# Attention's first batch: three head pairs in two halves of blocks, the first halves of all of them first

## The chip, the core and the metric

The kernel runs on one core of a Trainium2 chip. The time is device microseconds of one execution; a lower number is better.

## What is computed

The reference is a windowed attention followed by two gated layers. The weights come as 64-bit floats, q, k and v as 32-bit floats.

```
q, k, v: (4 batches, 8 heads, 576 tokens, 64)
scores = q @ k^T / 8, ALiBi slope per head, only 0 <= query - key < 128
x  = softmax(scores) @ v                  # to (2304 tokens, 512)
x  = (silu(x @ w_gate) * (x @ w_val)) @ w_out      # 512 -> 1536 -> 512
g  = x @ w_in;  out = (g * cos(g)) @ w_out2        # 512 -> 2048 -> 512
```

## The kernel before, in words

**Attention.** Two heads make a pair `u`; there are 16 pairs, four in each batch, and pairs 0 to 3 are the first batch. A pair's 576 tokens are four blocks of 128 (`NB = 4`) and a tail of 64. An item `(u, h, i)` is one block `i` of head `h`; the tails of both heads are one more item, `i = NB`. So a pair has nine items, and there are 144. A program loop, `for n in range(...)`, goes over them, and in round `n` it writes instructions for items at different stages: scores on TensorE (`do_s`, tiles `s`, L512), bias and row maximum on VectorE (`do_bias`, L520), exponential on ScalarE two items later (`do_exp`, L529), sum, reciprocal and scaling (L535, L541, L554 on GpSimd), transposes on TensorE five items later (`do_t`, L573; L563 in the later batches), a copy to SBUF by ScalarE (`do_hi`, L591), and attention times v eight or nine items later (`do_pv`, tile `pv` at L631, the tail at L605 and L607). ScalarE then writes the result's high part `xh` (L637) and VectorE its rest `xl` (L640). Every engine runs its own instructions in the written order.

**A pair's preparation** stands in the rounds of the pair before it: q is loaded and turned (`prep_t`, L449) and scaled to `qx` (`prep_q`, L455), the tail is turned (L461, L469, L471), k is turned and copied to `kx` (`prep_k`, L458). All loads are issued by SyncE in written order (`load_qk` L391 and L396, six issues; `load_v` L407 and L411, three issues). `nat1` holds two pairs' q and k, `nat2` two pairs' v, and `qk` two pairs' turned q and k.

**Weights.** A generator, `convert` (one step per round), turns the 64-bit weights into pairs of 32-bit parts, nine tiles of 512 KB: gate 0, val 0, gate 1, val 1, gate 2, val 2, out 0, out 1, out 2. Each is loaded by SyncE into one of two buffers `st` (L95, L100) and begins on ScalarE with L130 and L132, goes over VectorE (L133 to L145) and GpSimd (L152, L167) and ends as `wh` and `wl`.

**The filler.** Between attention's instructions TensorE gets work of the next layer: a generator of steps, each of three matmuls (L84, L85, L86). A batch has 72 steps (`STEPS`) in two jobs. The first batch's first job takes tokens 0 to 255: 12 steps of gate (`a_l1`), 12 of val and 12 of out (`a_l2`). Its first eight gate steps go by pairs of heads, and two of them run as soon as `ready` holds that pair, that is, when `xh` and `xl` of its tokens 0 to 255 are written. The second job needs the whole batch (`release`). `run_fill` writes at most what has come due; at most 1.6 steps come due in a round (`RATE`), and while a batch is worked on, `rate` spreads the steps that are left evenly over the rounds until the next batch is released. What remains after attention runs behind it, and then come the remaining layers, which the change does not touch.

**What sets the order in the first batch.** Pairs follow one another, nine items each. Only pair 3 (`u == NP - 1`) multiplies by v in two parts: tokens 0 to 255 when its first four items are through, then the rest. The stage distances are constants (`TRANS`, `HIGH`, `PVS`), one or two less for pair 3.

Of the kernel before, what the change touches and what calls it, by code (L numbers as in the profile page):

```python
# [9 lines left out]
F32 = mybir.dt.float32  # L10
F32R = mybir.dt.float32r
U32 = mybir.dt.uint32
AF = mybir.ActivationFunctionType
# [15 lines left out]
def kernel(  # L29
# [12 lines left out]
    nc = tc.nc  # L42
# [358 lines left out]
    def load_v(u):  # L401
        if u >= U:
            return
        b, p = divmod(u, NP)
        t = nat2.tile([128, NB, 2, D], F32, tag="v", name="v")
        for h in range(2):
            nc.sync.dma_start(  # L407
                out=t[:, :NB, h, :],
                in_=v[b, 2 * p + h, :NB * 128, :].rearrange("(n s) d -> s n d", s=128),
            )  # L410
        nc.sync.dma_start(  # L411
            out=vtail[u % 3][128 - TAIL:], in_=v[b, 2 * p:2 * p + 2, NB * 128:, :].rearrange("h s d -> s h d")
        )
        nat["v", u] = t


    vtail = [const.tile([128, 2, D], F32, name=f"vtail{j}") for j in range(3)]
    for t in vtail:
        nc.vector.memset(t[:128 - TAIL], 0.0)
    load_qk(0)  # L420
# [4 lines left out]
    load_v(0)  # L425
    ident = const.tile([128, 128], F32, name="ident")
    make_identity(nc, ident)
    qtx = [const.tile([128, 128], F32, name=f"qt{j}") for j in range(2)]
# [35 lines left out]
    def prep_tail(u):  # L464
        ps = PQ.pop((u, "t"))
        KT[u] = qk_p.tile([128, S], F32, tag="kx", name="kx")
        for j in range(2):
            r = slice(64 * j, 64 * j + 64)
            nc.scalar.activation(out=qtx[u % 2][r, r], in_=ps[r, 0:64], func=AF.Copy,  # L469
                                 scale=qscale[r, u % NP:u % NP + 1])  # L470
        nc.scalar.copy(out=KT[u][:, NB * 128:S], in_=ps[:, 64:128])  # L471

    items, first, final = [], {}, {}
    for u in range(U):
        for i in range(0, NB, 2):
            for h in range(2):
                items += [(u, h, i), (u, h, i + 1)]
        items.append((u, 0, NB))
        for j in range(0, NI, 2):
            g = list(range(u * NI + j, u * NI + min(j + 2, NI)))  # L480
            first[g[0]] = final[g[-1]] = g
    N = len(items)
    E, ST, PT, SP, TT, FT = {}, {}, {}, {}, {}, {}

# [3 lines left out]
    def do_s(groups):  # L488


        todo = []
        for g in groups:
            ps = ps_s.tile([128, 512], F32, tag="s", name="s")
            st = stats[stat_turn[0] % len(stats)]
            stat_turn[0] += 1
            at, ops = 0, []
            for m, n in enumerate(g):
                u, h, i = items[n]
                w = width(i)
                o = ps[:, at:at + w]  # L500
                at += w
                if i == NB:
                    ops.append((o, qtx[u % 2], KT[u][:, S - w:S]))
# [78 lines left out]
    def do_hi(g):  # L582
        ps = PT.pop(g[0])
        u, h, i = items[g[0]]
        if i == NB:
            nc.scalar.copy(out=ptt, in_=ps)
            return
        if i == 0:
# [9 lines left out]
    def do_pv(n):  # L598
        u, h, i = items[n]
        b_, p = divmod(u, NP)  # L600
        if i == NB:
            vt = nat["v", u]
            ps = (pm.tile([128, 512], F32, tag="pm", name="pm") if u == NP - 1 else
                  ps_q.tile([128, 512], F32, tag="pq", name="pq"))[:, :128]
            nc.tensor.matmul(out=ps, lhsT=vt[:, NB - 1].rearrange("p h d -> p (h d)"),  # L605
                             rhs=ptt[:, 0:128], start=True, stop=False)
            nc.tensor.matmul(out=ps, lhsT=vtail[u % 3].rearrange("p h d -> p (h d)"),  # L607
                             rhs=ptt[:, 128:256], start=False, stop=True)

            def fin():  # L610
# [67 lines left out]
    def last_pair(n):  # L678

        return 0 <= n < N and items[n][0] == NP - 1  # L680

    def staged(n, late, early):

        if last_pair(n - early) and n - early in final:
            return final[n - early]
        return None if last_pair(n - late) else final.get(n - late)
    for n in range(N + PVS + 2):
        pace = rate(n, due) if n < N else 1.5 * RATE
        due += 0.7 * pace
        u, idx = divmod(n, NI)  # L690
        v1 = u + 1 if u + 1 < U else None

        def ended(j):
            return final.get(n - j)

        todo = list(post)
        post.clear()
        if u < U and idx in AHEAD:
            do_s([first[u * NI + j] for j in AHEAD[idx]])
        turned, high = staged(n, TRANS, 4), staged(n, HIGH, 5)  # L700
        if high:
            do_hi(high)
        for m in first.get(n - EXP, ()):
            do_exp(m)
        for m in first.get(n if idx == NI - 1 else n - 1, ()) if idx else ():
            do_bias(m)
        if ended(NORM):
            do_guard(ended(NORM))
        if turned:
            do_t(turned)  # L710
        if v1 is not None:
            if idx == TT0:
                g = turned
                prep_tail_t(v1, TT[g[0]] if g else ps_t.tile([128, 512], F32, tag="t", name="t"))
        if ended(NORM):
            do_recip(ended(NORM))
            for m in ended(NORM):
# [2 lines left out]
            fn()  # L720
        due -= run_fill(int(due))
        due += 0.3 * pace
        for back in (PVS + 1, PVS, PVS - 2):
            for m in (ended(back) or ())[-1:]:
                u_, h_, i_ = items[m]
                if (h_ == 1 and (i_ == NB - 1 or i_ == 1 and last_pair(m)) or i_ == NB) and back == (
                        PVS - 2 if last_pair(m) else PVS if i_ == NB - 1 else PVS + 1):
                    do_pv(m)
        if v1 is not None:
            if idx == Q0 + 1:  # L730
                prep_q(v1)
            if idx == Q0:
                prep_t(v1, "q")
            if idx == K0:
                prep_t(v1, "k")
            if idx == K0 + 1:
                prep_k(v1)
            if idx == TT0 + 1:
                prep_tail(v1)
            if idx == max(TT0, K0) + 1:  # L740
                load_qk(u + 2)
            if idx == 7:
                load_v(u + 1)
        pdue = min(pdue + 1.0, 1.0)
        while pool_bg and pdue > 0:
            cost, fn = pool_bg.popleft()
# [556 lines left out]
```

## Time and profile before

| | |
|---|---|
| median of 3 runs | 984.19 us (983.91 to 987.03) |
| the profiled execution | 987.27 us, its span 985.2 us |
| mean granted TensorE clock in it | 0.990 |
| TensorE busy | 962.3 us, 98% |
| ScalarE, VectorE, GpSimd busy | 594.9, 731.0, 483.5 us |

A busy share is a mean over stages with different limits, and the busy time of matmuls counts their pipeline's length, so a TensorE that is busy to 90% can still be waiting. The granted clock is in shares of 2.4 GHz: 0.50 is the level of 1.2 GHz. Idle time stands with the instruction that ended it.

### The profile page before, as it was taken

Reading aid. Unit: us, or ns where it says so; the run is one execution under the profiler, and the core shown is the slowest. Engines: PE = TensorE matmul, PEld = TensorE weight load, DVE = VectorE, ACT = ScalarE, POOL = GpSimd, SP = SyncE. Lnnn points to the kernel's source line nnn. Section 1 sums busy time; section 2 is a strip of 40 time slices with the busy share of each in tenths; the row PEclk is TensorE's granted clock in tenths of the full one; section 3 lists DMA queues with packets and bytes.
Section 4 is the critical chain, followed back from the end, with each engine's and each line's share of the span. In section 5 each row is a group of like instructions: output and inputs, shape, how many; then the busy total and the mean of one; then the engine's idle time right before and its main releaser. Section 6 shows DMA issues by size and latency. Waiting matters only on the chain.

```text
span 985.2 us, 17051 instructions
## 1 busy us (share of the span) xinstructions
PE 962.3 (98%) x5620; PEld 884.6 (90%) x5620; DVE 731.0 (74%) x1549; ACT 594.9 (60%) x1366; POOL 483.5 (49%) x567
## 2 busy tenths in 40 slices
PE   6889999999999999999999999999999999999998
PEld 4658888889999999999999999888988888888886
DVE  6767777766288988989989755889666796666664
ACT  6876666653254545555545433878677776777663
POOL 5666645652245667769679721544232442323221
PEclk8889999999999999999999999999999999999999
DMA  7531352322383646647557625865767656576552
GB/s 181 157 92 42 95 123 68 85 75 70 110 281 107 204 128 223 205 130 252 172 164 240 193 89 177 296 201 182 245 201 229 201 161 203 181 247 202 164 180 86
DMA packets 145159, 163.65 MB, mean 166 GB/s; under 512 B 64688, under 2 KB 105648, under 8 KB 144816
## 3 DMA queue, kind: packets, MB, share of 16 engines
q1 hardware_dynamic: 143872, 162.27, 52.6%
q8 instruction: 45, 0.74, 0.3%
q10 hardware_dynamic: 1200, 0.30, 0.1%
q14 instruction: 42, 0.34, 0.1%
HBM read 126.88 MB, written 35.65 MB: 165 GB/s over the span
## 4 chain that ended last, share of the span: by engine, by line
PE 91%; DVE 3%; ACT 2%; DMA 2%; issue 1%; SPq 1%; POOL 0%; DVEq 0%; POOLq 0%; ACTq 0%
PE l L86 13%; PE l L85 13%; PE l L84 13%; PE pm L84 8%; PE pm L85 8%; PE pm L86 8%; PE pm L1028 6%; PE pm L1029 6%; PE pm L1027 5%; PE s L512 3%; PE pv L631 3%; PE pq L449 1%; PE t L563 1%; PE t L573 1%; ACT e L529 1%
## 5 line engine op out<-in xcount | busy, mean ns | idle before, releaser
L1152 POOL TENSOR_TENSOR r<-r,c 128x384 f32<-128x384 f32 x96 | 105.1, 1095 | 248.9 <-ACT r L1150 163.3
L84 PE MATMUL pm<-xh,wh 128*128 128x384 f32 (+3 forms) x456 | 153.4, 336 | 1.5 <-ACT fu L263 1.5
L85 PE MATMUL pm<-xl,wh 128*128 128x384 f32 (+3 forms) x456 | 145.9, 320 | 0.0
L86 PE MATMUL pm<-xh,wl 128*128 128x384 f32 (+3 forms) x456 | 145.9, 320 | 0.0
L86 PE MATMUL l<-wo,hl 128*128 128x512 f32 x288 | 114.2, 396 | 0.0
L85 PE MATMUL l<-wo,hh 128*128 128x512 f32 x288 | 113.7, 395 | 0.0
L84 PE MATMUL l<-wo,hh 128*128 128x512 f32 x288 | 112.1, 389 | 1.2 <-DMA wo<-wod 1.2
L843 POOL TENSOR_TENSOR cs<-cs,st 128x512 uint32<-128x512 uint32 x56 | 79.6, 1421 | 56.9 <-DVE cs L841 49.8
L1028 PE MATMUL pm<-xl,ws 128*128 128x384 f32 x318 | 107.4, 338 | 0.0
L1029 PE MATMUL pm<-xh,ws 128*128 128x384 f32 x318 | 106.8, 336 | 0.0
L1027 PE MATMUL pm<-xh,ws 128*128 128x384 f32 x318 | 106.2, 334 | 0.0
L84 PEld LDWEIGHTS pm<-xh,wh 128*128 128x128 f32 x456 | 86.3, 189 | 6.0 <-issue 2.7
L554 POOL TENSOR_SCALAR e<-e,st 128x128 f32<-128x128 f32 (+1 forms) x144 | 61.1, 427 | 62.1 <-DVE st L541 42.1
L85 PEld LDWEIGHTS pm<-xl,wh 128*128 128x128 f32 x456 | 86.4, 190 | 0.0
L86 PEld LDWEIGHTS pm<-xh,wl 128*128 128x128 f32 x456 | 86.2, 189 | 0.0
L1142 ACT ACTIVATE a<-c 128x384 f32<-128x384 f32 x96 | 49.8, 519 | 53.1 <-DVE c L1168 53.1
L529 ACT ACTIVATE e<-e,st 128x256 f32<-128x256 f32 (+1 forms) x144 | 68.1, 475 | 19.0 <-DVE st L520 13.5
L1147 DVE SCALAR_TENSOR_TENSOR r<-a,r 128x384 f32<-128x384 f32 x96 | 76.7, 799 | 3.3
L1149 ACT ACTIVATE r<-r 128x384 f32<-128x384 f32 x96 | 50.5, 526 | 41.3 <-DVE r L1147 41.3
L84 PE MATMUL l<-uh,wh 128*128 128x384 f32 x216 | 72.6, 336 | 0.7 <-DVE acc L968 0.5
L86 PE MATMUL l<-uh,wl 128*128 128x384 f32 x216 | 72.2, 334 | 0.0
L85 PE MATMUL l<-ul,wh 128*128 128x384 f32 x216 | 72.2, 334 | 0.0
(177 smaller groups left out, 2604.9 us busy)
## 6 DMA issues: line engine op xcount, KB each, us to landing
ws<-wid SPq DMA_DIRECT2D x168, 256.0 KB, 2.8
wo<-wod SPq DMA_DIRECT2D x48, 512.0 KB, 5.2
st<-in_moe_w_out_dram SPq DMA_DIRECT2D x28, 512.0 KB, 3.8
st<-in_moe_w_in_dram SPq DMA_DIRECT2D x16, 512.0 KB, 3.7
st<-in_moe_w_gate_dram SPq DMA_DIRECT2D x12, 512.0 KB, 4.2
st<-in_moe_w_val_dram SPq DMA_DIRECT2D x12, 512.0 KB, 3.8
wid<-sh SPq DMA_DIRECT2D x24, 256.0 KB, 4.0
wid<-sl SPq DMA_DIRECT2D x24, 256.0 KB, 3.5
```

Source lines behind the costliest of these rows:

```text
L84: nc.tensor.matmul(out=ps, lhsT=ah, rhs=bh, start=start, stop=False)
L85: nc.tensor.matmul(out=ps, lhsT=ah, rhs=bl, start=False, stop=False)
L86: nc.tensor.matmul(out=ps, lhsT=al, rhs=bh, start=False, stop=stop)
L529: nc.scalar.activation(out=e[:, :w], in_=e[:, :w], func=AF.Exp, bias=st[:, m:m + 1], scale=-1.0, accum_out=st[:, 2 + 2 * m:3 + 2 * m])
L554: nc.gpsimd.tensor_scalar(e[:, :w], e[:, :w], st[:, 8 + m:9 + m], 1.0, ALU.mult, ALU.mult)
L843: nc.gpsimd.tensor_tensor(out=ti, in0=ti, in1=st[:, :, 0], op=ALU.add)
L1027: nc.tensor.matmul(out=o, lhsT=wh, rhs=xh_, start=start and kk == 0, stop=False, skip_group_check=True)
L1028: nc.tensor.matmul(out=o, lhsT=wh, rhs=xl_, start=False, stop=False, skip_group_check=True)
L1029: nc.tensor.matmul(out=o, lhsT=wl, rhs=xh_, start=False, stop=kk == 1, skip_group_check=True)
L1147: nc.vector.scalar_tensor_tensor(out=r, in0=a, scalar=-C2, in1=r, op0=ALU.mult, op1=ALU.add)
L1149: nc.scalar.activation(out=r, in_=r, func=AF.Abs)
L1152: nc.gpsimd.tensor_tensor(out=r, in0=r, in1=h, op=ALU.mult)
```

## The change

The items of pairs 1 to 3 are put in another order: the first halves (blocks 0 and 1 of both heads, four items) of pairs 1, 2 and 3, then their second halves (blocks 2 and 3 and the tail, five items each). Each half is multiplied by v by itself. Pair 0 and the batches behind it keep their order. Preparation and loads of the first pairs stand in tables of rounds now, and more buffers hold what lives longer: v, turned q and k, and tails of four pairs. The number of items, of loads and of filler steps stays.

```diff
-    nat2 = att.enter_context(tc.tile_pool(name="nat2", bufs=2))
-    qk_p = att.enter_context(tc.tile_pool(name="qk", bufs=2))
+    nat2 = att.enter_context(tc.tile_pool(name="nat2", bufs=4))
+    qk_p = att.enter_context(tc.tile_pool(name="qk", bufs=4))
...
-    items, first, final = [], {}, {}
-    for u in range(U):
-        for i in range(0, NB, 2):
+    items, first, final, part, scores = [], {}, {}, {}, {}
+    HB = NB // 2
+    order = [(0, 0, NB + 1)] + [(u, *c) for c in ((0, HB), (HB, NB + 1)) for u in range(1, NP)]
+    for u, b0, b1 in order + [(u, 0, NB + 1) for u in range(NP, U)]:
+        base = len(items)
+        for i in range(b0, min(b1, NB), 2):
             for h in range(2):
                 items += [(u, h, i), (u, h, i + 1)]
...
-        lo, hi = (0, NB * 128) if u != NP - 1 else (0, HA) if i == 1 else (HA, NB * 128)
+        lo, hi = part[n][0] * 128, min(part[n][1], NB) * 128
...
-    AHEAD = {0: (0, 2), 4: (4, 6), 7: (8,)}
-    Q0, K0, TT0 = 2, 5, 4
+    Q0, K0, TT0 = {1: 2, 2: 8, 3: 12, 4: 28}, {1: 5, 2: 11, 3: 15, 4: 31}, {1: 4, 2: 10, 3: 14, 4: 30}
+    LQ, LV = {2: 1, 3: 6, 4: 20, 5: 33}, {1: 7, 2: 10, 3: 14, 4: 34}
+    for u in range(NP + 1, U):
+        Q0[u], TT0[u], K0[u] = ((u - 1) * NI + j for j in (2, 4, 5))
+        LV[u] = (u - 1) * NI + 7
+        if u + 1 < U:
+            LQ[u + 1] = (u - 1) * NI + 6
...
+    def lag(n):
+
+        u, _, i = items[n]
+        if u in (0, *range(NP, U)):
+            return TRANS, HIGH, PVS + (i == NB)
+        if u == NP - 1 or part[n][0] == 0:
+            return TRANS - 1, HIGH - 1, PVS - 2
+        return TRANS, HIGH, PVS - 1 + (u == 1 and i == NB)
...
-            ps = (pm.tile([128, 512], F32, tag="pm", name="pm") if u == NP - 1 else
+            ps = (pm.tile([128, 512], F32, tag="pm", name="pm") if NP - 2 <= u < NP else
```

What the tables hold: `Q0`, `K0` and `TT0` are the rounds in which a pair's q, k and tail are turned, `LQ` and `LV` those in which its loads are issued. Before, q and k of pairs 2 and 3 were loaded in rounds 6 and 15 and turned from rounds 11 and 20 on.

**SyncE's queue.** Its issues at the start, from pair 0's tail of v to the weight tile val 1. Before:

```order
L411 DMA vtail_128<-in_v_dram 64x2x64
L95 DMA st<-in_moe_w_gate_dram 128x4x256
L391 DMA q<-in_q_dram 128x4x64 x2
L391 DMA k<-in_k_dram 128x4x64 x2
L396 DMA qkt<-in_q_dram 64x2x64
L396 DMA qkt<-in_k_dram 64x2x64
L407 DMA v<-in_v_dram 128x4x64 x2
L411 DMA vtail_129<-in_v_dram 64x2x64
L95 DMA st<-in_moe_w_val_dram 128x4x256
```

The same place in the change, from behind pair 0's tail of v:

```order
L391 DMA q<-in_q_dram 128x4x64 x2
L391 DMA k<-in_k_dram 128x4x64 x2
L396 DMA qkt<-in_q_dram 64x2x64
L396 DMA qkt<-in_k_dram 64x2x64
L95 DMA st<-in_moe_w_gate_dram 128x4x256
L391 DMA q<-in_q_dram 128x4x64 x2
L391 DMA k<-in_k_dram 128x4x64 x2
L396 DMA qkt<-in_q_dram 64x2x64
L396 DMA qkt<-in_k_dram 64x2x64
L407 DMA v<-in_v_dram 128x4x64 x2
L411 DMA vtail_129<-in_v_dram 64x2x64
L95 DMA st<-in_moe_w_val_dram 128x4x256
```

Pair 2's six issues moved ahead of the tile gate 1, and pair 3's six stand between gate 1 and val 1.

**TensorE in rounds 29 and 30.** The names are tiles (`pm` and `xh`, `wh` the filler's, `t` transposed exponentials, `s` scores). Before, the block of filler steps that is shown stands in round 39, between the turning of pair 5's q (round 38) and the scores of round 40:

```order
L449 MATMUL pq<-ident,q 128x128 x4
L573 MATMUL t<-ident,e 128x128 x2
L84 MATMUL pm<-xh,wh 128x256
L85 MATMUL pm<-xl,wh 128x256
L86 MATMUL pm<-xh,wl 128x256
L84 MATMUL pm<-xh,wh 128x256
L85 MATMUL pm<-xl,wh 128x256
L86 MATMUL pm<-xh,wl 128x256
L84 MATMUL pm<-xh,wh 128x256
L85 MATMUL pm<-xl,wh 128x256
L86 MATMUL pm<-xh,wl 128x256
L512 MATMUL s<-kx,qx 128x256 x4
```

In the change it stands in round 29, behind the scores of pair 2's tail:

```order
L520 MATMUL s<-kx,qt_169 128x192
L581 MATMUL t<-ident,e 128x128 x4
L84 MATMUL pm<-xh,wh 128x256
L85 MATMUL pm<-xl,wh 128x256
L86 MATMUL pm<-xh,wl 128x256
L84 MATMUL pm<-xh,wh 128x256
L85 MATMUL pm<-xl,wh 128x256
L86 MATMUL pm<-xh,wl 128x256
L84 MATMUL pm<-xh,wh 128x256
L85 MATMUL pm<-xl,wh 128x256
L86 MATMUL pm<-xh,wl 128x256
L581 MATMUL t<-ident,e 128x128 x2
```

The block of three steps with which the filler gets going (its seventh to ninth step) moved from round 39 to round 29.

**TensorE around the end of the first batch.** In the change, from pair 3's second product with v (round 41) to the filler's 25th step (round 43); its 24th stands in round 39:

```order
L639 MATMUL pv<-pth_974,v 64x128
L639 MATMUL pv<-pth_1021,v 64x128
L639 MATMUL pv<-pth_974,v 64x256
L639 MATMUL pv<-pth_1021,v 64x256
L639 MATMUL pv<-pth_974,v 64x128
L639 MATMUL pv<-pth_1021,v 64x128
L613 MATMUL pm<-ptt,v 128x128
L615 MATMUL pm<-ptt,vtail_131 128x128
L449 MATMUL pq<-ident,k 128x128 x4
L571 MATMUL t<-ident,e 128x128 x2
L520 MATMUL s<-kx,qt_167 128x192
L84 MATMUL pm<-fh,wh 128x256
```

In these rounds the filler has nothing to write: its next 12 steps need the tile out 2, which is converted in round 43 in both kernels. After round 43 the program has 15 steps before and 26 in the change; at the end of round 82 both have 73.

## Rows read from the trace of the kernel before

**Rows 1.** The page: TensorE in slices of 24.6 us; the chain that ended last.

```profile
PE   6889999999999999999999999999999999999998
...
PE 91%; DVE 3%; ACT 2%; DMA 2%; issue 1%; SPq 1%; POOL 0%; DVEq 0%; POOLq 0%; ACTq 0%
```

**Rows 2.** Busy time by stretch: PE, PEld, DVE, ACT, POOL; clock, DMA share, GB/s.

```profile
10.00:20.00 10.00, 8.16 (x34) 5.36 (x34) 8.58 (x35) 8.18 (x26) 6.25 (x9) 0.95 0.89 220
8.00:66.00 58.00, 48.57 (x277) 33.68 (x278) 46.34 (x168) 48.97 (x152) 39.00 (x56) 0.86 0.62 155
60.00:70.00 10.00, 7.92 (x41) 5.69 (x39) 5.26 (x25) 5.78 (x20) 4.91 (x8) 0.67 0.27 62
74.00:140.00 66.00, 65.18 (x507) 55.66 (x509) 48.11 (x205) 42.85 (x151) 39.32 (x92) 1.00 0.34 83
```

**Rows 3.** TensorE by stretches of 2 us: busy, granted clock, DMA share, GB/s.

```profile
62.00:64.00 2.00, 0.57 (x3) 0.86 0.62 141
64.00:66.00 2.00, 1.61 (x8) 0.50 0.07 16
...
68.00:70.00 2.00, 2.00 (x10) 0.50 0.00 0
70.00:72.00 2.00, 2.00 (x20) 0.93 0.03 8
```

**Rows 4.** Timeline of TensorE: filler steps at half and full clock, a product with v.

```profile
59.67 0.87 PE L631 MATMUL pv<-pth,v 128*64 128x256 f32 x8
...
63.77 0.56 PE L84 MATMUL pm<-xh,wh 128*128 128x256 f32 x1
...
64.56 0.41 PE L84 MATMUL pm<-xh,wh 128*128 128x256 f32 x1
...
77.17 0.39 PE L84 MATMUL pm<-xh,wh 128*128 128x256 f32 x1
...
77.99 0.38 PE L563 MATMUL t<-ident,e 128*128 128x128 f32 x2
```

**Rows 5.** Timeline of ScalarE; in brackets idle time before and its end's cause.

```profile
17.99 0.67 ACT L130 ACTIVATE ct<-st 128x512 f32<-128x512 f32 x1
...
23.55 0.67 ACT L130 ACTIVATE ct<-st 128x512 f32<-128x512 f32 x1 [0.28 <-POOL e L554]
...
50.71 0.68 ACT L130 ACTIVATE ct<-st 128x512 f32<-128x512 f32 x1 [0.79 <-DMA st<-in_moe_w_out_dram]
...
71.14 0.37 ACT L637 CAST xh<-pv 128x256 fp32r<-128x256 f32 x1 [4.00 <-PE pv L631]
71.41 0.63 ACT L469 ACTIVATE qt<-t,qscale 64x64 f32<-64x64 f32 x2
...
73.72 0.38 ACT L263 ACTIVATE fu<-pm 128x256 f32<-128x256 f32 x1
...
74.47 0.43 ACT L265 ACTIVATE th<-fu 128x256 f32<-128x256 f32 x1
...
82.31 0.63 ACT L469 ACTIVATE qt<-t,qscale 64x64 f32<-64x64 f32 x2
...
85.96 0.59 ACT L637 CAST xh<-pv 128x512 fp32r<-128x512 f32 x1 [1.21 <-PE pv L631]
```

**Rows 6.** Timeline of SyncE's issues.

```profile
10.73 0.60 SPq L411 DMA_DIRECT2D vtail<-in_v_dram  x1
12.25 0.37 SPq L95 DMA_DIRECT2D st<-in_moe_w_gate_dram  x1
12.72 1.24 SPq L391 DMA_DIRECT2D q<-in_q_dram  x2
...
16.74 0.62 SPq L396 DMA_DIRECT2D qkt<-in_k_dram  x1
...
19.30 0.53 SPq L95 DMA_DIRECT2D st<-in_moe_w_val_dram  x1
```

**Rows 7.** Transfers into the weight tiles `st`, 0 to 75 us.

```profile
DMA to landing us min/median/max: 3.5/3.7/5.3
```

More of the change, by code (lines that the diff above doesn't have):

```diff
@@ L411, in load_v @@
         nc.sync.dma_start(
-            out=vtail[u % 3][128 - TAIL:], in_=v[b, 2 * p:2 * p + 2, NB * 128:, :].rearrange("h s d -> s h d")
+            out=vtail[u % 4][128 - TAIL:], in_=v[b, 2 * p:2 * p + 2, NB * 128:, :].rearrange("h s d -> s h d")
         )
         nat["v", u] = t
-    vtail = [const.tile([128, 2, D], F32, name=f"vtail{j}") for j in range(3)]
+    vtail = [const.tile([128, 2, D], F32, name=f"vtail{j}") for j in range(4)]
     for t in vtail:
@@ L427 @@
     make_identity(nc, ident)
-    qtx = [const.tile([128, 128], F32, name=f"qt{j}") for j in range(2)]
+    qtx = [const.tile([128, 128], F32, name=f"qt{j}") for j in range(4)]
     for t in qtx:
@@ L468, in prep_tail @@
             r = slice(64 * j, 64 * j + 64)
-            nc.scalar.activation(out=qtx[u % 2][r, r], in_=ps[r, 0:64], func=AF.Copy,
+            nc.scalar.activation(out=qtx[u % 4][r, r], in_=ps[r, 0:64], func=AF.Copy,
                                  scale=qscale[r, u % NP:u % NP + 1])
         nc.scalar.copy(out=KT[u][:, NB * 128:S], in_=ps[:, 64:128])
-    items, first, final = [], {}, {}
-    for u in range(U):
-        for i in range(0, NB, 2):
+    items, first, final, part, scores = [], {}, {}, {}, {}
[4 more added lines that the diff above has]
+        for i in range(b0, min(b1, NB), 2):
             for h in range(2):
                 items += [(u, h, i), (u, h, i + 1)]
-        items.append((u, 0, NB))
-        for j in range(0, NI, 2):
-            g = list(range(u * NI + j, u * NI + min(j + 2, NI)))
+        if b1 > NB:
+            items.append((u, 0, NB))
+        count = len(items) - base
+        for j in range(0, count, 2):
+            g = list(range(base + j, base + min(j + 2, count)))
             first[g[0]] = final[g[-1]] = g
+            part[g[-1]] = b0, b1
+            ahead = j if j == count - 1 else j // 4 * 4
+            scores.setdefault(base + ahead - (1 if ahead == j == count - 1 else 0), []).append(g)
     N = len(items)
@@ L587, in do_hi @@
             return
-        if i == 0:
+        if i == part[g[-1]][0]:
             pth[u, h] = big.tile([128, NB * 256], F32, tag=f"pth{h}", name=f"pth{h}")
@@ L673, with staged @@
     EXP, NORM, TRANS, HIGH, PVS = 2, 2, 5, 6, 8
-    AHEAD = {0: (0, 2), 4: (4, 6), 7: (8,)}
-    Q0, K0, TT0 = 2, 5, 4
-    due = pdue = 0.0
[L678 to L686, printed above, removed]
+    Q0, K0, TT0 = {1: 2, 2: 8, 3: 12, 4: 28}, {1: 5, 2: 11, 3: 15, 4: 31}, {1: 4, 2: 10, 3: 14, 4: 30}
[5 more added lines that the diff above has]
+            LQ[u + 1] = (u - 1) * NI + 6
+    Q0, K0, TT0, LQ, LV = ({n: u for u, n in t.items()} for t in (Q0, K0, TT0, LQ, LV))
+    due = pdue = 0.0
+    def lag(n):
[5 more added lines that the diff above has]
+        return TRANS, HIGH, PVS - 1 + (u == 1 and i == NB)
+    def staged(n, stage):
+        for j in range(TRANS - 1, PVS + 2):
+            if n - j in final and lag(n - j)[stage] == j:
+                return final[n - j]
+        return None
     for n in range(N + PVS + 2):
@@ L697 @@
         post.clear()
-        if u < U and idx in AHEAD:
-            do_s([first[u * NI + j] for j in AHEAD[idx]])
-        turned, high = staged(n, TRANS, 4), staged(n, HIGH, 5)
+        if n in scores:
+            do_s(scores[n])
+        turned, high = staged(n, 0), staged(n, 1)
         if high:
@@ L704 @@
             do_exp(m)
-        for m in first.get(n if idx == NI - 1 else n - 1, ()) if idx else ():
-            do_bias(m)
+        for m in [*first.get(n - 1, ()), *first.get(n, ())]:
+            if (items[m][2] == NB) == (m == n):
+                do_bias(m)
         if ended(NORM):
@@ L710 @@
             do_t(turned)
[L711 to L714, printed above, removed]
+        if n in TT0:
+            room = turned and items[turned[0]][2] in (0, NB) and not folded(turned[0])
+            prep_tail_t(TT0[n], TT[turned[0]] if room else ps_t.tile([128, 512], F32, tag="t", name="t"))
         if ended(NORM):
@@ L722 @@
         due += 0.3 * pace
[L723 to L743, printed above, removed]
+        valued = staged(n, 2)
+        if valued and (items[valued[-1]][2] == NB or items[valued[-1]][1] == 1 and
+                       items[valued[-1]][2] == min(part[valued[-1]][1], NB) - 1):
+            do_pv(valued[-1])
+        for at, act in ((n - 1, prep_q), (n, prep_t)):
+            if at in Q0:
+                act(Q0[at], "q") if act is prep_t else act(Q0[at])
+        if n in K0:
+            prep_t(K0[n], "k")
+        if n - 1 in K0:
+            prep_k(K0[n - 1])
+        if n - 1 in TT0:
+            prep_tail(TT0[n - 1])
+        if n in LQ:
+            load_qk(LQ[n])
+        if n in LV:
+            load_v(LV[n])
         pdue = min(pdue + 1.0, 1.0)
```

6 lines of the change are left out of this document (2 added, 4 removed).

## The prediction

> **What bounds the kernel now.** The page comes first: the chain that ended last runs on TensorE for 91% of the span, and TensorE's slices are full from the fifth on; only the first four, some 98 us, show 6, 8, 8 and 9 tenths [rows 1]. So time can only be won in the first tenth of the run, and what is won there is worth something only if it leaves less work for TensorE behind it. The second view is the busy time by stretch. From 8 to 66 us ScalarE is busy for 48.97 of 58 us and TensorE for 48.57, at a mean clock of 0.86; from 74 to 140 us TensorE has 65.18 of 66 us at full clock, and ScalarE, VectorE and GpSimd have 42.85, 48.11 and 39.32 [rows 2]. So there are two stages: up to about 72 us (round 42, in which the first batch is released) a round is set by ScalarE and by waits along its chain, and behind it by TensorE alone, while the others have a quarter or more to spare. The third view is the same in steps of 2 us: TensorE is busy for 0.57 of 2 us at 62 to 64 us, its granted clock then falls to 0.50 (1.2 GHz), and it has full clock again from about 70 us [rows 3]. In that stretch ScalarE stands still for 4.00 us until pair 3's second product with v is through [rows 5].
>
> **The change part by part.**
>
> *Filler steps that move.* Counted in the order of the instructions, 26 steps stand in the program after round 43 in the change and 15 before; by round 82 both have 73. So 11 steps leave the stage that TensorE sets and go into rounds 29 to 39 of the first stage. At full clock two steps take 77.17 to 77.99, 0.41 us each [rows 4], and 11 × 0.41 = 4.5 us come off the second stage. That holds if the other engines follow in shorter rounds. They did where the rounds were short: from round 41 to 50, 71.41 to 82.31, nine items took 10.9 us, 1.21 us each, with 13 steps among them [rows 5]. From 74 to 140 us the mean is longer, and with 1.19 instead of 1.49 steps due per round (`rate`) a round gets 0.3 × 0.41 = 0.12 us shorter; the busiest of the others, VectorE, has 48.11 of 66 us [rows 2], so it follows. I take −4.5; the bounds are −4.5 and −2.3, half of it, if chains between the engines take the rest.
>
> *SyncE's queue.* This is the price that I take most seriously. The tile gate 1 was issued at 12.25 us. Now six issues for pair 2 stand ahead of it; in the trace they took from 12.72 to 17.36 us, 4.64 us [rows 6]. They can begin when the tail of v is issued, at 11.33 [rows 6], so gate 1 is issued at about 16.0. A weight tile lands 3.5 to 5.3 us behind its issue [rows 7]: 19.5 to 21.3. ScalarE took it up at 17.99 with no wait [rows 5] and has the same instructions up to there, so it waits 1.5 to 3.3 us, with all later exponentials and copies behind it in its queue. The transfers' share was 0.89 from 10 to 20 us [rows 2], so I take a middle landing time and 2.2 us. The Trainium skill, "DMA: Bandwidth & Descriptors", section "Queues, rings and completion order", says that on each DMA engine descriptors are consumed in ring order, so pair 2's bytes go ahead of gate 1's as well; by that rule the upper end would be right, and the sum would be 1.1 us higher. No row here separates issue from ring. Val 1 comes behind six issues for pair 3 and three for v: 16.0 + 0.4 + 4.6 + 1.8 = 22.8, landing at 26.5 with the median. ScalarE wanted it at 23.55 [rows 5], now 2.2 later and behind pair 2's tail (0.63 + 0.21), which makes 26.6: no second wait, or up to 1.6 if it lands as late as 5.3. Together +2.2, between 0 (ScalarE has 9 us of idle time from 8 to 66 us [rows 2] that could take it up) and +4.9.
>
> *The queue later.* Loads of v no longer wait for a buffer, and pairs 2 and 3 are loaded by then, so the tile out 1, for which ScalarE waited 0.79 us at 50.71 [rows 5], comes in time: −0.8, between −0.8 and 0.
>
> *More work for ScalarE in the first stage.* The third gate tile's copy and tanh (0.38 and 0.43, now behind the stage, at 73.72 [rows 5]) come into it: 0.8. Pairs 1 and 2 get two copies of 256 columns (0.37) for one of 512 (0.59), 0.15 each [rows 5]. That is 1.1 us, on an engine that is busy for 84% of the stage: I take +0.8, between 0 and 1.1. VectorE's like work is hidden behind ScalarE.
>
> *More work for TensorE there.* A product with v in two halves has 20 passes for 16, at 0.87/8 = 0.11 each [rows 4]: 0.4 us for each of two pairs, and the 11 steps. From 8 to 66 us TensorE is idle for 9.4 us [rows 2], and that covers the 0.9 us; it costs that much if the cover is gone. For the steps see the clock. Pair 2's and pair 3's scores now stand one round behind the copy of `kx` instead of three: 0 to 1 us, and I take 0, since a round of other work lies between.
>
> *The clock.* At half clock a first step takes 63.77 to 64.56, 0.79 us, against a mean of 0.41 [rows 4]. The half-clock stretch of some 6.6 us before 70.2 [rows 3] costs up to 3.3 us where TensorE sets the pace. Rounds 29 to 39 get more for TensorE to do, so that the lull before such a stretch may be filled; but a step stands behind the same waits in TensorE's queue, and rounds 40 to 42 have no step at all. Bounds: −3.3 (the stretch is gone) and +3.3 (one more, where rounds 40 to 42 are empty). I take −1.0, a third of the gain, because the lull at 62 to 64 us falls into rounds that now have steps.
>
> *What costs nothing:* three more memsets at the start, where VectorE waits for the first transposes, and the larger pools. The stages behind attention get the same instructions.
>
> *The sum:* −4.5 + 2.2 − 0.8 + 0.8 − 1.0 = −3.3 us. Against the profiled execution (987.27 us, of which 985.2 are the span and 2.1 lie around it) that is 984.0; that execution ran 3.1 us above the median of the runs shown, 984.19. For the median I forecast **980.9 us**.
>
> **The rivals.**
>
> *A. The clock stays up* from round 29 until the release, and ScalarE's 4.00 us wait [rows 5] shrinks with it. Then the clock term is −3.3: the sum is −5.6, **978.6 us**. For it speaks that the dense stretch behind the release, from 74 to 140 us, keeps 1.00 throughout [rows 2]; against it the empty rounds 40 to 42. The Trainium skill, "TensorE: Matmul & The Clock Gate", Part 1, has the slow level as the default that activity releases; by that rule the added steps would bring exactly this, and the fall behind the lull at 62 us agrees with it.
>
> *B. The steps are paid where they now stand.* If TensorE sets the rounds 29 to 42, at either clock, the first stage grows by about the 4.5 us that the second loses, and the queue and ScalarE's work remain: −4.5 + 4.5 + 2.2 − 0.8 + 0.8 = +2.2, **986.4 us**, or no change if the queue is hidden. This is the case in which the change doesn't do what it says: the filler's work goes on at an earlier item, but not at an earlier time. For it speaks that from 64 to 70 us TensorE is busy throughout and ScalarE waits for it [rows 3, 5]; against it the 9.4 us of idle time before.
>
> *C. SyncE's queue decides, and the kernel is slower.* If not only gate 1 but also val 1 comes late by what the queue puts ahead of it (issued at 22.8 instead of 19.3, 3.5 us) and both land at the slow end (1.6 us more than the median), ScalarE loses 3.3 + 3.5 + 1.6 = 8.4 us: with the other terms (clock 0) −4.5 + 8.4 − 0.8 + 0.8 = +3.9, **988.1 us**. It decides from a loss of about 7.5 us on. For it speaks the DMA share of 0.89 [rows 2]; against it that val 1 is wanted later too once gate 1 was late.
>
> **How the numbers follow.** A measurement of this kernel can tell about 0.3%, 2.95 us, from no change: below 981.2 is faster, above 987.1 slower. The forecast gets 0.45, A 0.20, B 0.22, C 0.13. The forecast's own range, 978.9 to 983.1, lies somewhat more than half below 981.2. Faster: 0.26 + 0.20 = 0.46. Slower: 0.13 from C and 0.03 from B's upper end, 0.16. Same: 0.38. The range from 977.8 to 986.5 reaches over A's time and B's and leaves out C and the ends, less than 2 in 10.
>
> **What would show it.** In the profile of the changed kernel: ScalarE's third L130 with a wait of some 2 us for a gate tile at about 20 us, and no wait at the tile out 1; the filler's block of three steps at about 50 us instead of 64; the release still at 71 to 74 us; rounds of the second batch shorter by a tenth of a microsecond, with TensorE still without gaps; and everything behind it shifted by the same 3 us. The prediction is wrong if the first batch's release comes more than 4 us later (B or C, told apart by whether TensorE or the weight tiles are waited for), or more than 2 us earlier (A or something that I don't see).

## The result and the profile after

The changed kernel takes 990.44 us (median of 5 runs, 989.52 to 991.40), the kernel before 985.08 us (5 runs): 1.0057 times as long, with an interval of 1.0046 to 1.0068. It is slower; the forecast was 980.9 us. The execution of before whose rows stand above came out some 2 us over that median, so in what follows differences of times come from medians and differences of places from traces. Places in the changed kernel therefore look up to 2 us less late than they would against a usual execution of before.

The page of the kernel after, TensorE in slices of 24.7 us and the chain that ended last:

```profile
PE   5789999999999999999999999999999999999998
...
PE 88%; DVE 6%; ACT 2%; DMA 1%; issue 1%; POOL 0%; SPq 0%; DVEq 0%; POOLq 0%; ACTq 0%
```

Against [rows 1] the loss is where it was looked for, in the first slices (5 and 7 for 6 and 8), but VectorE's part of the chain has doubled, from 3 to 6%. Busy time by stretch (columns as in rows 2), first the stretch that answers to [rows 2], then those that answer to [rows 3], then 20 to 30 us:

```profile
74.00:140.00 66.00, 64.69 (x486) 54.05 (x486) 48.08 (x207) 44.41 (x156) 39.72 (x94) 1.00 0.37 88
...
62.00:64.00 2.00, 2.00 (x19) 1.98 (x18) 2.00 (x6) 1.96 (x9) 0.93 (x2) 1.00 0.73 164
64.00:66.00 2.00, 1.30 (x12) 0.98 (x10) 1.92 (x11) 1.98 (x6) 1.05 (x3) 1.00 0.40 92
...
20.00:30.00 10.00, 4.52 (x26) 2.88 (x25) 5.65 (x19) 8.23 (x26) 5.36 (x8) 0.70 0.80 206
```

The last stretch in the kernel before:

```profile
20.00:30.00 10.00, 9.38 (x55) 6.59 (x55) 9.63 (x34) 8.99 (x28) 8.40 (x12) 0.71 0.61 166
```

The stretch at half clock at 64 us is gone: TensorE has 3.30 of the 4 us from 62 to 66, and the granted clock is 1.00. At 20 to 30 us the clock is as low as before (0.70 and 0.71), but TensorE has only 4.52 us of work there instead of 9.38, so it mostly stands still while pairs 2 and 3 are prepared. By stretches of 2 us, TensorE has the half clock for some 20 us of the first 76 before (19 to 26, 36 to 43 and 64 to 70 us) and for some 10 us in the change (24 to 31 and 48 to 51 us). From 74 to 140 us the row shows half a microsecond less busy time than before, but with the stretch moved by the 4.1 us of the shift (78.1 to 144.1) it is 65.05 of 66 us against 65.18. SyncE's issues and ScalarE (answering to [rows 6] and [rows 5]):

```profile
15.30 0.54 SPq L95 DMA_DIRECT2D st<-in_moe_w_gate_dram  x1
...
21.96 0.53 SPq L95 DMA_DIRECT2D st<-in_moe_w_val_dram  x1
```

```profile
19.45 0.68 ACT L130 ACTIVATE ct<-st 128x512 f32<-128x512 f32 x1 [1.29 <-POOL e L562]
...
53.52 0.65 ACT L130 ACTIVATE ct<-st 128x512 f32<-128x512 f32 x1
...
75.23 0.37 ACT L645 CAST xh<-pv 128x256 fp32r<-128x256 f32 x1 [0.89 <-PE pv L639]
75.50 0.63 ACT L469 ACTIVATE qt<-t,qscale 64x64 f32<-64x64 f32 x2
```

Gate 1 is issued 3.05 us later and ScalarE takes it up 1.46 us later (the row names GpSimd, but the tile landed only 4.1 us behind its issue, at 19.4 us, and experiment 4's row names the tile); the tile out 1 is there when it is wanted; round 41, 71.41 before, is now at 75.50.

To follow the loss through the run I take the starts of the 144 exponentials on ScalarE, counted from 0, since every kernel here has the same number of them. Numbers 40, 85 and 141 before:

```profile
72.28 0.51 ACT L529 ACTIVATE e<-e,st 128x256 f32<-128x256 f32 x1
...
134.77 0.51 ACT L529 ACTIVATE e<-e,st 128x256 f32<-128x256 f32 x1
...
213.13 0.51 ACT L529 ACTIVATE e<-e,st 128x256 f32<-128x256 f32 x1
```

The same in the change:

```profile
76.38 0.51 ACT L537 ACTIVATE e<-e,st 128x256 f32<-128x256 f32 x1
...
135.81 0.51 ACT L537 ACTIVATE e<-e,st 128x256 f32<-128x256 f32 x1
...
215.89 0.51 ACT L537 ACTIVATE e<-e,st 128x256 f32<-128x256 f32 x1
```

It is 4.10 us late at number 40, 1.04 at number 85 and 2.76 at number 141; the span ends 3.7 us later. So the second stage does give time back, but 3.1 us instead of 4.5, and from number 85 on 1.7 us are lost again, although both programs have the same items and the same filler steps there.

### The profile page after: what moved, and what is told of

It is laid out like the page before. It is cut to its first block, busy times and chain, and to the rows that moved or that the text cites. A ratio compares the mean times of both kernels' runs of the same rounds, so it can differ in the third digit from the quotient of the medians.

```text
span 988.9 us, 17023 instructions
## 1 busy us (share of the span) xinstructions
PE 961.9 (97%) x5628; PEld 884.5 (89%) x5628; DVE 731.5 (74%) x1554; ACT 595.4 (60%) x1368; POOL 483.5 (49%) x567
## 4 chain that ended last, share of the span: by engine, by line
PE 88%; DVE 6%; ACT 2%; DMA 1%; issue 1%; POOL 0%; SPq 0%; DVEq 0%; POOLq 0%; ACTq 0%
PE l L85 13%; PE l L86 13%; PE l L84 13%; PE pm L84 8%; PE pm L85 7%; PE pm L86 7%; PE pm L1042 6%; PE pm L1043 5%; PE pm L1041 5%; PE s L520 4%; PE pv L639 3%; PE pq L449 1%; PE t L571 1%; PE t L581 1%; DMA wo<-wod 1%
## 5 line engine op out<-in xcount | busy, mean ns | idle before, releaser
L562 POOL TENSOR_SCALAR e<-e,st 128x128 f32<-128x128 f32 (+2 forms) x144 | 60.4, 424 | 71.8 <-DVE st L549 59.7
L537 ACT ACTIVATE e<-e,st 128x256 f32<-128x256 f32 (+2 forms) x144 | 67.9, 473 | 31.3 <-DVE st L543 18.4
```

The lines of the kernel that those rows point to most:

```text
L537: nc.scalar.activation(out=e[:, :w], in_=e[:, :w], func=AF.Exp, bias=st[:, m:m + 1], scale=-1.0, accum_out=st[:, 2 + 2 * m:3 + 2 * m])
L562: nc.gpsimd.tensor_scalar(e[:, :w], e[:, :w], st[:, 8 + m:9 + m], 1.0, ALU.mult, ALU.mult)
```

## The experiments

Theory at first: the squeezed preparation of pairs 2 and 3 costs the time. Rivals: SyncE's queue; the steps paid where they now stand; the larger buffers. A later theory, the order on VectorE, came out of the traces of the first seven kernels and is tested by the last five. "Before" is the kernel before, run beside it on the same chip. Behind "Measured" stand the median, the ratio to before and its 95% interval.

**1. Gate 1 ahead of pair 2's loads.**

```diff
-    LQ, LV = {2: 1, 3: 6, 4: 20, 5: 33}, {1: 7, 2: 10, 3: 14, 4: 34}
+    LQ, LV = {2: 3, 3: 6, 4: 20, 5: 33}, {1: 7, 2: 10, 3: 14, 4: 34}
```

> The change, with pair 2's q and k loaded two rounds later, so that they stand behind the tile gate 1 in SyncE's queue as before. In the changed kernel ScalarE's third L130 starts 1.5 us later than before (19.45 instead of 17.99) and the first batch is 4.1 us late at round 41. Queue theory: the late tile starts the loss; the third L130 goes back to about 18.0, and the kernel gains 1.5 us or more, to about 988.9 us or less. Theory of the bank (q of pair 3 waits for the only bank pq, and through it for ScalarE): the loss of 4 us in rounds 9 to 17 stays, no more than 0.5 to 1 us is gained, 989.5 to 990. Theory that the moved filler steps are paid in rounds 29 to 40: no gain beyond 1.5 us either.

Measured: 992.14 us against 985.52, 1.0071 (1.0059 to 1.0083). Exponential 6, up to which the tile gate 1 matters, is in time again (0.28 us late instead of 1.48), but number 13 is 6.88 us late instead of 4.82. Most of these 2.06 us is again a late tile: val 1, issued at 24.12 instead of 21.96 us, for which ScalarE waits ahead of the copy to pair 2's `kx`:

```profile
28.16 0.66 ACT L130 ACTIVATE ct<-st 128x512 f32<-128x512 f32 x1 [1.53 <-DMA st<-in_moe_w_val_dram]
```

So the experiment exchanges one late tile for another. It shows that gate 1 in time is no cure, and not that late tiles cost nothing; what the queue costs is read from experiment 4.

**2. A PSUM bank of their own for the turned q of pairs 2 and 3** (`pm` instead of the single `pq`).

```diff
-                act(Q0[at], "q") if act is prep_t else act(Q0[at])
+                act(Q0[at], "q", pm if Q0[at] in (2, 3) else None) if act is prep_t else act(Q0[at])
```

> The change, with the turned q of pairs 2 and 3 in a bank of the filler's pool pm, which is free in these rounds, instead of the one bank pq. Bank theory: TensorE's wait of 3.2 us at pair 3's q (for ScalarE's copy kx of pair 2) goes away, VectorE's 2.9 us wait for the scores behind it too, and the kernel gains 2 to 3.5 us: 987 to 988.5. Queue theory: the wait moves to the scores, which need kx of pair 2 all the same, and the gain is under 0.7 us. Steps theory: no gain at the end, since rounds 29 to 40 take up what comes earlier.

Measured: 989.67 us, 1.0041 (1.0028 to 1.0054): 0.8 us under the change, which the two intervals do not tell from nothing. The wait moved on to the scores that need `kx`.

**3. The moved steps held back:** the filler's seventh step waits for round 39, and pair 2's tail product is back in `pq`.

```diff
-                while kk not in ready or ("g", 1) not in g0:
+                while kk not in ready or ("g", 1) not in g0 or kk == KD - 1 and rnd[0] < 39:
```

> The change, with the filler held at its seventh step until round 39, as before; order of the items, tables and loads stay (pair 2's tail product goes back to the bank pq, since the held banks of the filler are needed). If the moved steps lie in idle time and the second stage gains what it showed (3.1 us), this kernel loses 3 us against the change: about 993.5 us. If the steps are paid where they now stand, it is as fast as the change or faster: 987.5 to 990.5, and rounds 29 to 40 get shorter by 3 us or more.

Measured: 994.26 us, 1.0091 (1.0078 to 1.0104), 3.8 us more than the change. The steps that move are a gain of that size in this kernel. Without them exponential 40 is 1.95 us late instead of 4.10, so about half of their cost is paid again in the first stage, but number 85 is 3.89 us late instead of 1.04. As to the end, rival B is refuted.

**4. The early loads alone, in the kernel before** (loads in the change's rounds, four buffers for v).

```diff
+            if n in (1, 6, 24):
+                load_qk({1: 2, 6: 3, 24: 4}[n])
+            if n in (10, 14):
+                load_v({10: 2, 14: 3}[n])
```

> The kernel before with nothing but the change's order of loads: q and k of pairs 2 and 3 in rounds 1 and 6, v of pairs 2 and 3 in rounds 10 and 14, with four buffers for v. Queue theory: gate 1 comes 1.5 us late here too, val 1 somewhat, and the kernel is 1 to 2.5 us slower than before (986 to 987.5). Bank and steps theories: pair 2's and 3's turns stand late as before, so ScalarE makes up for it and the time is that of before within 0.7 us; the wait for the tile out 1 (0.79 us) may even go.

Measured: 987.33 us, 1.0016 (1.0008 to 1.0025), 1.8 us. The queue costs about what the forecast put on it (2.2), and nothing is lost behind exponential 85.

**5. The buffers alone, in the kernel before.**

```diff
-    qk_p = att.enter_context(tc.tile_pool(name="qk", bufs=2))
+    qk_p = att.enter_context(tc.tile_pool(name="qk", bufs=4))
...
-    qtx = [const.tile([128, 128], F32, name=f"qt{j}") for j in range(2)]
+    qtx = [const.tile([128, 128], F32, name=f"qt{j}") for j in range(4)]
```

> The kernel before with the change's buffers alone (four instead of two of the natural v, of qx and kx and of the turned tails, four instead of three value tails); order, loads and filler stay. The change runs 5.4 us over before, and a part of that comes after the 85th exponential, where both programs have the same order: the scores of blocks 2 and 3 of a pair take 1.13 us for eight before, 1.17 to 1.54 after. Theory layout (other addresses and later reuse of the buffers slow those scores): 987.5 to 988.5 us, nothing up to the 85th exponential, then 2 to 3 us. Theory squeeze (the loss is made in rounds 9 to 28, where two pairs are prepared close together, and the later loss is the state that this leaves the engines in): 985.5 us, within 0.8 of before, scores at 1.13.

Measured: 984.51 us against 985.13, 0.9996 (0.9987 to 1.0004): no difference. The layout is not the cause.

**6. The weights' conversion out of the way of the preparation.**

```diff
-        next(pieces, None)
+        for _ in range(0 if 8 <= n < 14 else 2 if 24 <= n < 36 else 1):
+            next(pieces, None)
```

> The change with the conversion of the first weight tiles standing still in rounds 8 to 13 and taking two steps a round in rounds 24 to 35, so that tile val 1's loads and ScalarE's L130 leave the rounds in which pairs 2 and 3 are prepared; the filler's steps stand where the change has them from round 25 on. Theory squeeze, with the weights' work as the other half of it: kx of pair 2 no longer stands behind val 1's L130 on ScalarE; the 13th to 28th exponentials come 2 to 4 us earlier against the change, and the end 986.5 to 988.5 us. Rival, the pairs' own loads and turns are the limit (q and k of two pairs on one queue by 20 us): the 13th exponential within 1 us of the change's, and the end 990 to 991 us. Rival, the same work is only paid later, in rounds 24 to 35 where the steps stand: early exponentials gain, the end 990 us.

Measured: 990.48 us, 1.0055 (1.0039 to 1.0070), no gain on the change. Exponential 13 came 3.6 us earlier than in the change, as the theory wanted, and number 39 was 7.93 us late all the same: rounds 29 to 39 took it back. TensorE there, in this kernel:

```profile
49.85 0.28 PE L86 MATMUL pm<-xh,wl 128*128 128x256 f32 x1
53.40 0.39 PE L84 MATMUL pm<-xh,wh 128*128 128x256 f32 x1 [3.28 <-ACT fu L263]
```

A filler step waits 3.28 us for its bank, which ScalarE has to empty (L263) behind the weights' work, and everything behind it on TensorE waits too. So the squeeze in rounds 9 to 17 is not the whole of it.

**7. The second pair whole,** only the third and fourth in halves, with loads, turns and v moved to match; the filler goes on at item 34.

```diff
-    order = [(0, 0, NB + 1)] + [(u, *c) for c in ((0, HB), (HB, NB + 1)) for u in range(1, NP)]
+    order = [(u, 0, NB + 1) for u in range(2)] + [(u, *c) for c in ((0, HB), (HB, NB + 1)) for u in range(2, NP)]
...
-    Q0, K0, TT0 = {1: 2, 2: 8, 3: 12, 4: 28}, {1: 5, 2: 11, 3: 15, 4: 31}, {1: 4, 2: 10, 3: 14, 4: 30}
-    LQ, LV = {2: 1, 3: 6, 4: 20, 5: 33}, {1: 7, 2: 10, 3: 14, 4: 34}
+    Q0, K0, TT0 = {1: 2, 2: 11, 3: 15, 4: 28}, {1: 5, 2: 13, 3: 18, 4: 31}, {1: 4, 2: 12, 3: 17, 4: 30}
+    LQ, LV = {2: 6, 3: 11, 4: 22, 5: 33}, {1: 7, 2: 15, 3: 19, 4: 34}
```

> The change with the second pair (pair 1) kept whole and only the third and fourth in halves: pairs 2 and 3 are needed from items 18 and 22 instead of 13 and 17, their loads start at rounds 6 and 11 instead of 1 and 6, and the filler goes on at item 34 instead of 29; 23 of its steps stand by the end of round 43 (15 before, 26 with the change). Theory squeeze: with the preparation spread out the early loss goes (13th exponential within 1 us of before, 40th within 3), 8 of 11 steps still leave the later rounds, worth 8/11 of the 3.8 us measured by holding them: 982.5 to 985 us. Rival, halves cost in themselves (more value products, later-stage scores that no longer overlap, 2 to 3 us after the 85th exponential): 986.5 to 989 us.

Measured: 990.15 us, 1.0053 (1.0040 to 1.0066). The preparation was spread out, exponential 13 was 1.50 us late instead of 4.82, and the kernel was as slow as the change. The theory of the squeeze alone falls.

**What the seven had in common.** Behind exponential 85 all five traces of kernels with the change's loop (the change and experiments 1, 2, 3, 6) lost between 1.72 and 1.77 us up to number 141, experiment 7 lost 2.13, and experiments 4 and 5, with the loop of before, lost nothing. Five kernels with different first stages and one and the same loss speak for an order, not for a state that the first stage leaves behind. The timeline of VectorE at the change of pairs, first in the kernel before, then in the change:

```profile
138.56 0.69 DVE L640 TENSOR_TENSOR xl<-pv,xh 128x512 fp32r<-128x512 f32 x1
139.21 0.16 DVE L535 TENSOR_REDUCE st<-st 128x2 f32<-128x4 f32 x1
139.41 0.17 DVE L541 RECIPROCAL st<-st 128x2 f32<-128x2 f32 x1
139.54 0.46 DVE L268 SCALAR_TENSOR_TENSOR fu<-th,fu 128x288 f32<-128x288 f32 x1
140.43 0.46 DVE L616 TENSOR_TENSOR xl<-pq,xh 64x64 fp32r<-64x64 f32 x2 [0.43 <-ACT xh L614]
140.92 0.29 DVE L520 CUSTOM_DVE_ANT_0 e<-s,rel 128x128 f32<-128x128 f32 x1
```

```profile
139.59 0.69 DVE L648 TENSOR_TENSOR xl<-pv,xh 128x512 fp32r<-128x512 f32 x1
141.95 0.42 DVE L528 CUSTOM_DVE_ANT_0 e<-s,rel 128x256 f32<-128x256 f32 x1 [1.68 <-PE s L520]
142.30 0.08 DVE L528 DVE_READ_ACCUMULATOR2_ANT st<- 128x1 f32 x1
142.30 0.15 DVE L543 TENSOR_REDUCE st<-st 128x2 f32<-128x4 f32 x1
142.49 0.17 DVE L549 RECIPROCAL st<-st 128x2 f32<-128x2 f32 x1
142.57 0.44 DVE L268 SCALAR_TENSOR_TENSOR fu<-th,fu 128x288 f32<-128x288 f32 x1
142.93 0.45 DVE L624 TENSOR_TENSOR xl<-pq,xh 64x64 fp32r<-64x64 f32 x2
143.41 0.29 DVE L528 CUSTOM_DVE_ANT_0 e<-s,rel 128x128 f32<-128x128 f32 x1
```

The bias of the new pair starts when its scores are there, 1.03 us later than before, as everything is at this point. But before, it is the first item's (128x128), and sum, reciprocal, SiLU and `xl` are done while the scores are made. In the change it is the second item's (128x256), it stands ahead of those four, and they run behind it. The first item's bias starts at 143.41, 2.49 us behind that of before. It comes from this part of the diff, which is not among the lines shown ahead of the forecast:

```diff
-        for m in first.get(n if idx == NI - 1 else n - 1, ()) if idx else ():
-            do_bias(m)
+        for m in [*first.get(n - 1, ()), *first.get(n, ())]:
+            if (items[m][2] == NB) == (m == n):
+                do_bias(m)
```

`first` gives the two items of a group at its first item. Before, both get their bias one round later. In the change, an item `m` that is no tail passes where `m != n`: the first item in the round after, but the second, `n + 1`, already in round `n`, in which the scores of half of the groups have only just been written. This holds in all 16 pairs.

**8. The bias in the order of before, the rest as in the change.**

```diff
-            if (items[m][2] == NB) == (m == n):
+            if (items[m][2] == NB) == (n in first and m in first[n]):
```

> The change with one line of its loop put back to the rule of before: both items of a group get their bias on VectorE one round after the group's first item. In the change as it stands the second item of a group gets its bias a round earlier, in the round in which the group begins and ahead of the first item's, in all 16 pairs; the diff of the loop holds this, and the forecast did not price it. Seen in the trace: behind the 85th exponential every kernel with the new order loses the same 1.7 to 2.1 us up to the 141st, those with the old loop nothing, and in front of it VectorE waits 1.68 us for scores at 141.95 us with sum, reciprocal and xl queued behind. Theory bias order: the loss of 1.7 us behind the 85th exponential goes (within 0.3 of none), rounds 9 to 40 gain 1 to 4 us as well, and the end is 984 to 988 us. Rival, phase (the engines keep a state from the squeezed first stage, and the line is innocent): the later loss stays, 989 to 991 us.

Measured: 983.95 us against 985.29, 0.9986 (0.9974 to 0.9999). One line takes 6.5 us off the change (6.7 when each is taken against before beside it). Exponentials 40, 85 and 141:

```profile
73.19 0.51 ACT L537 ACTIVATE e<-e,st 128x256 f32<-128x256 f32 x1
...
130.64 0.51 ACT L537 ACTIVATE e<-e,st 128x256 f32<-128x256 f32 x1
...
209.00 0.51 ACT L537 ACTIVATE e<-e,st 128x256 f32<-128x256 f32 x1
```

They stand 0.91 us behind, 4.13 ahead and 4.13 ahead of before. So the line costs 3.2 us up to number 40 (4.10 - 0.91), 2.0 up to number 85 and 1.7 behind it. These two executions lie 7.7 us apart in their spans, the medians 6.5, so the first of the three may be some 1 us too high. VectorE's bias group over five pairs (busy, mean of one, idle time ahead of it and its causes), in the kernel before, the change and this one:

```profile
L520 DVE CUSTOM_DVE_ANT_0 e<-s,rel 128x256 f32<-128x256 f32 (+1 forms) x39 | 13.9, 386 | 2.3 <-PE t L563 1.2 <-PE s L512 0.9
```

```profile
L528 DVE CUSTOM_DVE_ANT_0 e<-s,rel 128x256 f32<-128x256 f32 (+1 forms) x40 | 14.7, 386 | 7.8 <-PE s L520 7.4 <-PE t L571 0.2
```

```profile
L528 DVE CUSTOM_DVE_ANT_0 e<-s,rel 128x256 f32<-128x256 f32 (+1 forms) x39 | 13.9, 387 | 2.1 <-PE t L571 1.0 <-PE s L520 0.9
```

The wait for scores ahead of the bias is 0.9, 7.4 and 0.9 us. TensorE shows it in its scores, which go into banks that the late bias has yet to read (see the last section): the six groups of scores of blocks 2 and 3 between exponentials 85 and 141 take 6.79 us before and in this kernel, and 8.25 in the change, 1.46 of the 1.7 us. Between 40 and 85 five of them take 5.99 us here and 7.20 in the change, 1.2 of the 2.0. In the first stage it costs as well; VectorE in the change and in this kernel, at the turning of pair 3's q:

```profile
26.79 0.43 DVE L133 TENSOR_SCALAR ct<-ct 128x512 f32<-128x512 f32 x1 [1.07 <-ACT ct L130]
30.12 0.42 DVE L528 CUSTOM_DVE_ANT_0 e<-s,rel 128x256 f32<-128x256 f32 x1 [2.90 <-PE s L520]
30.47 0.08 DVE L528 DVE_READ_ACCUMULATOR2_ANT st<- 128x1 f32 x1
30.47 0.75 DVE L455 TENSOR_SCALAR qx<-pq,qscale 128x512 f32<-128x512 f32 x1
```

```profile
29.04 0.75 DVE L455 TENSOR_SCALAR qx<-pq,qscale 128x512 f32<-128x512 f32 x1 [1.22 <-PE pq L449]
```

In the change `qx` of pair 3 stands behind a bias that waits 2.90 us, and starts 2.1 us after TensorE has turned q (28.40); here it starts as q is turned.

**9. The change's bias rule alone, in the kernel before** (the hunk above).

> The kernel before with the change's rule for the bias alone: the second item of each group a round earlier, everything else as before. Theory bias order: 987 to 990 us, 1.7 us or more of it behind the 85th exponential, with the scores of blocks 2 and 3 at 1.17 to 1.54 us instead of 1.13. Rival, phase: 985.5 us, within 0.8 of before, scores at 1.13.

Measured: 988.07 us against 985.29, 1.0027 (1.0018 to 1.0036), 2.8 us. Between exponentials 85 and 141 it loses 1.73 us, and the bias waits 7.4 us for scores, as in the change:

```profile
L520 DVE CUSTOM_DVE_ANT_0 e<-s,rel 128x256 f32<-128x256 f32 (+1 forms) x40 | 14.6, 387 | 7.7 <-PE s L512 7.4 <-PE t L563 0.2
```

The same six groups of scores take 8.24 us. The later loss is shown from both sides now. Numbers 40, 85 and 141 stand 4.43, 2.54 and 0.81 us ahead of before. Most of the 4.43 us is the two executions, before's 2.0 us above its median and this one's 1.4 below. But from 40 to 141 it loses 3.6 us, more than the 2.8 of the medians, so in this item order the rule cost nothing in the first stage.

**10. Experiment 7 with the bias in the order of before.**

> The kernel with the second pair whole and the bias in the order of before. Theory bias order: its 990.2 us lose the 2.1 us behind the 85th exponential and 1 to 3 us ahead of it: 984 to 987 us. Rival, phase: 989.5 to 991 us. If the order of the items is worth something once the bias is right, this kernel, whose preparation is spread out, comes out below 985.1.

Measured: 981.06 us against 985.29, 0.9962 (0.9948 to 0.9975): 9.1 us less than experiment 7, and faster than both kernels. Exponential 13 is 0.26 us late; number 40 is 3.76 us and number 85 7.12 us ahead of before. Between these two it gains 3.4 us with eight steps moved. Its tiles gate 1 and val 1 are issued at 12.35 and 18.69 us, about as before (12.25 and 19.30), so it goes without the queue's price, too.

**11. Experiment 6 with the bias in the order of before.**

> The change with the weights' conversion standing still in rounds 8 to 13 and the bias in the order of before. If the early squeeze costs by itself, this one is below the change with the bias alone put back, by up to the 0.5 us that the standing weights were worth with the wrong order, or more: 982 to 987 us; if the rounds 28 to 40 take back whatever comes in earlier, the two are equal within 1 us.

Measured: 987.77 us, 1.0026 (1.0016 to 1.0036), 3.8 us slower than experiment 8 and past the end of what was expected. Exponential 13 is 0.70 us late instead of 4.65, number 39 is 8.41 late instead of 5.18. The weights' work that was pushed back meets the filler's steps in rounds 29 to 39 and costs more there.

**12. Experiment 10 with the change's bias rule in rounds 0 to 41 alone.**

> The kernel with the second pair whole and the bias in the order of before, but with the change's early bias in rounds 0 to 41 alone. It tells whether the early bias harms in the first stage as well, where ScalarE sets the pace, or only where TensorE does. With the early bias throughout, the same item order took 990.2 us, 9.1 more than with the old rule; behind the 42nd round the traces of the two differ by some 5.7 us. Theory, the rule harms in both stages: 983 to 986 us. Rival, in the first stage it is free or a gain: 979.5 to 982 us.

Measured: 983.78 us against 985.01, 0.9998 (0.9982 to 1.0013), 2.7 us more than experiment 10, and the intervals lie apart. Number 40 is 0.66 us ahead of before instead of 3.76, and from there on the distance of 3.1 us to experiment 10 stays. With the halves the rule harms in the first stage too.

## Why the prediction was wrong

**The step that failed** is the one that puts VectorE at nothing. Of the first stage the forecast says that VectorE's "like work is hidden behind ScalarE", of the second that VectorE has 48.11 of 66 us, "so it follows". Both go by how long VectorE is busy; the order of its instructions was not gone through, and the hunk on `do_bias` got no price. The runs showed in its place a bias that waits for its scores ahead of ready work: the wait rose from 0.9 to 7.4 us over five pairs, and the line costs 6.5 us (experiment 8 against the change), more than the whole difference from before (5.4). With the line put back the time is 983.95 us, inside the forecast's range of 977.8 to 986.5 and 3 us above the time that it names.

**Filler steps that move,** forecast -4.5 us: right in mechanism and nearly in size. With the old bias rule the second stage gives 5.0 us (0.91 late to 4.13 ahead, experiment 8), 0.11 us a round where 0.12 was forecast, for eleven steps and 3.4 for eight (experiment 10). In the change VectorE took 2.0 of it, and 3.1 were left.

**SyncE's queue,** forecast +2.2 us: 1.8 by the early loads alone (experiment 4); the wait at the third L130 came as described, 1.46 us late. Experiment 1 only moved the wait from gate 1 to val 1. The tile out 1 came in time, as forecast. The 0.8 us for ScalarE's added work were not measured by themselves.

**Scores one round behind `kx`,** forecast 0 of 0 to 1 us: too low, with the rest of the squeeze. In experiment 8 exponential 13 is 4.65 us late, and TensorE waits for pair 2's `kx` before it can turn pair 3's q (both use the one bank `pq`):

```profile
27.89 1.11 PE L449 MATMUL pq<-ident,q 128*128 128x128 f32 x4 [4.30 <-ACT kx L458]
```

Experiment 10, with the preparation spread out, is 2.9 us faster than experiment 8 although it moves three steps fewer. That is about what the forecast's other terms fall short by: 980.9 against 983.95. But it also goes without the queue's price, so how much of it is the squeeze alone is not shown.

**The clock,** forecast -1.0 of -3.3 to +3.3 us: the forecast counted one stretch at half clock, 6.6 us in front of the release, while its own mean of 0.86 over 58 us [rows 2] comes to some 16 us at half clock. Two more stood at 19 to 26 and 36 to 43 us. In the change the one in front of the release went away, the one at 36 us made room for one of some 3 us at 48, and the first stayed, 5 us later, with TensorE waiting for `kx`. The half clock fell from some 20 to some 10 us, and the release was late all the same. What it is worth was not measured by itself.

**Of the rivals,** A's condition came true and its time did not. From round 29 (52 us) to the release the granted clock in the change is 1.00, ScalarE waits 0.89 us for pair 3's second product instead of 4.00, and the release is late all the same:

```profile
52.00:76.00 24.00, 21.27 (x175) 17.65 (x173) 19.05 (x71) 19.74 (x62) 16.64 (x25) 1.00 0.41 98
```

B fell with experiment 3, although some 2 us of the steps' cost are paid in the first stage. C's time (988.1) lies nearest, 2.3 us off and by another mechanism. The release was 4.1 us late, past the bound at which the forecast called itself wrong; of the two causes that it named for this neither was behind most of it, since the bias line alone takes 3.2 us off it (experiment 8).

Two things stay open: why the early bias is free in the first stage with the old item order (experiment 9) but not with the halves, and what makes up the last 0.9 us of the change's span, behind exponential 141.

## What to carry to other kernels

Where a change rewrites the loop that writes instructions, compare the order on every engine, also in the stages that it isn't about: one condition that put a waiting instruction four places ahead cost more than the reordering gained. An instruction that will wait belongs behind the work that is ready, since on an engine that runs in written order the wait is paid by all that stands behind it. And a loss of the same size in kernels with different histories points to an order in the program: undo the smallest part that they share.

## What was not expected of the hardware

The scores of two heads' blocks 2 and 3, four matmuls in eight passes into two banks, took 1.13 us when both banks were free. In the change they took up to 1.56 us without a wait being shown ahead of them. The matmuls take the two banks in turn, and by the times of the rows the second bank was freed while they ran. TensorE in the change, then in experiment 8:

```profile
145.59 1.54 PE L520 MATMUL s<-kx,qx 64*128 64x256 f32 x8
```

```profile
140.43 1.13 PE L520 MATMUL s<-kx,qx 64*128 64x256 f32 x8
```

The wait lies inside the group, where these rows show none: in the change, VectorE's last bias on that bank began at 145.65 us, behind the first of these matmuls, and its maximum was read at 145.86. The clock is 1.00 in both. A group of matmuls that grows longer at the same clock can thus be the only sign of a wait in such rows.
